# Grouped-query decode attention beside a mish layer: where the next pair's queries are spread, and which of VectorE's work stands first in the second unit

## The chip, the cores and the metric

The kernel runs on one core of one Trainium2 chip. The metric is device time in microseconds of one execution, the median of several runs. The profile is one execution more, taken by the hardware profiler.

## The reference

One decode step for 8 sequences of width 512. A layernormed input goes through cached attention with 32 query heads over 8 key/value heads (8192 cached positions, head size 128) and through a dense layer with mish; both are added to the input. All is float32.

```python
def _A_ref(x, k_cache, v_cache, wq, wo):
    q = (x @ wq).reshape(B, Sq, Hq, Dh).transpose(0, 2, 1, 3)
    k = jnp.repeat(k_cache, rep, axis=1)
    v = jnp.repeat(v_cache, rep, axis=1)
    scores = jnp.einsum("bhqd,bhkd->bhqk", q, k) * (Dh ** -0.5)
    p = softmax(scores, axis=-1)
    o = jnp.einsum("bhqk,bhkd->bhqd", p, v)
    return o.transpose(0, 2, 1, 3).reshape(B, Sq, Hq * Dh) @ wo

def _B_ref(x, w1, b1, w2):
    h = jnp.einsum("bsd,df->bsf", x, w1) + b1
    sp = jnp.log1p(jnp.exp(-jnp.abs(h))) + jnp.where(h > 0, h, jnp.zeros_like(h))
    return jnp.einsum("bsf,fd->bsd", h * jnp.tanh(sp), w2)

xn = layernorm(x)
return x + _A_ref(xn, ...) + _B_ref(xn, ...)
```

## The kernel before

The caches are the bulk: keys and values are 268 MB each, read once. The work is cut into 32 units. A unit is one sequence and one pair of key/value heads; a pair of heads has 8 units, one for each sequence, so there are 4 pairs. In the loop `j` is the unit, `b = j % 8` its place in the pair.

A unit's key tile and value tile are 8.39 MB each (128 partitions of 64 KB). They share one SBUF tile, `kv`, of 160 KB a partition. Values always lie at its start. Keys lie in two places that overlap by half: even units at `ROW`, odd units at `1.5 ROW`. So the keys of unit `j + 1` may be loaded only when the half of the keys of `j` that both places share has been used; `scores` therefore goes through that shared half first, and the load of the next keys is issued between the two halves of `scores`. All these loads go through SP's queue, in program order: the next keys wait for the first half of the scores, the next values for the values matmuls that still read the value place.

A unit runs in this order on each engine, as written in the loop (the order is by hand; the pools and the scheduler do not reorder it):

- `scores(j)`, line 279: 64 TensorE matmuls of a weight tile `wk` made from the queries against the keys, into one PSUM bank.
- `softmax(j)`, lines 291 to 312: row maximum on VectorE, two small TensorE transposes, the exponential on ScalarE, row sums.
- `values(j - 1)`, line 341: 64 TensorE matmuls of the previous unit's probabilities against its values, then four VectorE operations (lines 349 and 351) that gather the result.
- `key_weights(j + 1)`, line 262: two VectorE products that make the next unit's `wk` from the spread queries `qr`.
- `turn(j)`: TensorE matmuls (lines 318 and 319) that move the probabilities into four PSUM banks, then on VectorE the reciprocal (321), four transposes into `tr` (323) and two reduces into `pt8` (329).
- `merge(j - 1)`: one TensorE matmul (358) and a VectorE product (359).

Once in a pair the queries of the next pair are made: the weights are loaded at `b == 4` (`load_q`), projected at `b == 5` (`project`, lines 218 to 237), and spread. The spread is two steps: `selections` (line 205) copies a pattern from the identity into `wide`, which is the same memory as `tr`; `spread` (lines 244 and 251) runs two groups of 8 TensorE matmuls with that pattern as weights into two of the four PSUM banks that `turn` uses, each group followed by a ScalarE copy into `qr`. Before, both steps stand at the end of the unit with `b == 6`.

The first unit has no previous values. In their place it runs `mish`: TensorE matmuls (365, 370) and some 15 VectorE operations (378 to 404) that work in the memory in which the third unit's keys will be loaded.

Of the kernel before, what the change touches and what calls it, by code (L numbers as in the profile page):

```python
# [29 lines left out]
FG = F // G  # L30
# [26 lines left out]
W1_AT = ROW  # L57
# [1 line left out]
PLACES = 2 * ROW + ROW // 2  # L59


LOAD_Q, MAKE_Q, SPREAD_Q = 4, 5, 6


@with_exitstack
def kernel(
# [20 lines left out]
    kv = const.tile([P, PLACES], F32, name="kv")  # L87
# [26 lines left out]
    def load_q(m):  # L114

        rows = wq.rearrange("j p f -> (j p f)").rearrange("(m p f) -> m p f", m=NP, p=P)
        nc.sync.dma_start(ws, rows[m])

    def load_unit(src, j, at):
        m, b = divmod(j, B)  # L120
        lo = (b * HKV + 2 * m) * NH * G
        t = kv[:, at : at + ROW]
        nc.sync.dma_start(
            t,
            src[lo : lo + NB].rearrange("j p f -> (j p f)").rearrange("(p f) -> p f", p=P),
        )
        return t
# [5 lines left out]
    b1_sb = kv[:G, W1_AT + 7168 : W1_AT + 7168 + FG]  # L133
# [3 lines left out]
    w1_t = kv[:, W1_AT : W1_AT + 7168].rearrange("p (j f) -> p j f", j=2 * CC)  # L137
# [75 lines left out]
    def project():  # L213

        w = ws.rearrange("p (c f) -> p c f", c=CC)
        for d in range(2):
            for c in range(CC):
                nc.tensor.matmul(  # L218
                    H[Q * c : Q * c + B, :],
                    xn4[:, c, :],  # L220
                    w[:, c, d * 512 : (d + 1) * 512],
                    start=True,
                    stop=True,
                )
            qp = work.tile([P, 512], F32, name="e")
            nc.scalar.copy(qp, H)  # L226
            for h in range(REP):
                at = 192 + (d * REP + h) * B
                nc.tensor.matmul(  # L229
                    M[:, at : at + B],  # L230
                    qp[:, h * DH : (h + 1) * DH],
                    bsel[:, :B],
                    start=True,
                    stop=True,
                )
        qT = work.tile([P, H2 * B], F32, name="qT", bufs=1)
        nc.vector.tensor_scalar_mul(qT, M[:, 192 : 192 + H2 * B], DH**-0.5)
        return qT

    def spread(qT):  # L240

        for half in range(2):
            for k in range(8):
                nc.tensor.matmul(  # L244
                    X[:, half, k * 64 : (k + 1) * 64],
                    wide[:, half * 8 + k],
                    qT,
                    start=True,
                    stop=True,
                )  # L250
            nc.scalar.copy(  # L251
                qr[:, half * 8 : (half + 1) * 8].rearrange("p i c -> p (i c)"), X[:, half]
            )
# [3 lines left out]
    def key_weights(j):  # L257
        b = j % B
        w = WK[j] = work.tile([P, DI, 2, NH * G, REP], F32, name="wk", bufs=1)
        q = qr.rearrange("p i (d o h b) -> p i d o h b", d=2, o=1, b=B)[..., b]  # L260
        for d in range(2):
            nc.vector.tensor_mul(  # L262
                w[:, :, d],
                q[:, :, d].to_broadcast([P, DI, NH * G, REP]),
                mask[:, d * NH * G : (d + 1) * NH * G]
                .rearrange("p (o k r) -> p o k r", o=1, r=1)
                .to_broadcast([P, DI, NH * G, REP]),
            )


    def scores(j, k, first, part):

        w = WK[j]
        lo = 0 if first else DI // 2
        kk = k.rearrange("p (i c f) -> p i c f", i=DI, c=HALF)
        for n in range(DI // 2):
            i = lo + n
            for c in range(HALF):
                nc.tensor.matmul(  # L279
                    S[64 * c : 64 * (c + 1), :],  # L280
                    w[:, i].rearrange("p d k h -> p (d k h)"),
                    kk[:, i, c, :],
                    start=(part == 0 and n == 0),
                    stop=(part == 1 and n == DI // 2 - 1),
                )
# [51 lines left out]
    def values(j, vt):  # L337
        for n in range(NJ):
            l, c = divmod(n, HALF)
            q = n % G  # L340
            nc.tensor.matmul(  # L341
                O[Q * q : Q * (q + 1), :],
                pt8[:, c, TL * l : TL * (l + 1), :].rearrange("p t h -> p (t h)"),
                vt[:, 512 * n : 512 * (n + 1)],
                start=(n < G),
                stop=(n >= NJ - G),
            )
        os = work.tile([P, DH], F32, name="os")
        nc.vector.tensor_scalar(os, O[:, :DH], isel[:, 0:1], None, op0=ALU.mult)  # L349
        for i in range(1, TL):  # L350
            nc.vector.scalar_tensor_tensor(  # L351
                os, O[:, DH * i : DH * (i + 1)], isel[:, i : i + 1], os, op0=ALU.mult, op1=ALU.add
            )
        return os
# [7 lines left out]
    def mish(w1_t, b1_sb, flat):  # L362
        hp = H[:, :FG]
        for g in range(G):
            nc.tensor.matmul(
                hp[Q * g : Q * g + B, :], gsel[:, g, :], b1_sb, start=True, stop=False
            )
        for c in range(CC):
            for g in range(G):
                nc.tensor.matmul(  # L370
                    hp[Q * g : Q * g + B, :],
                    xnT[:, c, :],
                    w1_t[:, c * 2 + g // 2, g % 2 * FG : (g % 2 + 1) * FG],
                    start=False,
                    stop=(c == CC - 1),
                )
        a, z, z2, one, h = (flat[:, FG * i : FG * (i + 1)] for i in range(5))
        nc.vector.tensor_copy(h, hp)
        nc.vector.scalar_tensor_tensor(a, h, -1.0, h, op0=ALU.mult, op1=ALU.max)
        nc.scalar.activation(z, a, AF.Exp, scale=-1.0)  # L380
        nc.vector.tensor_mul(z2, z, z)
        m = a
        nc.vector.tensor_single_scalar(m, h, 0.0, op=ALU.is_gt)
        nc.vector.tensor_scalar(one, z2, -1.0, 1.0, op0=ALU.mult, op1=ALU.add)
        nc.vector.tensor_mul(one, one, m)
        t1 = m
        nc.vector.tensor_add(t1, one, z2)
        t2 = z2
        nc.vector.tensor_scalar(one, one, -1.0, 1.0, op0=ALU.mult, op1=ALU.add)
        nc.vector.scalar_tensor_tensor(t2, z, 2.0, t1, op0=ALU.mult, op1=ALU.add)  # L390
        nc.vector.scalar_tensor_tensor(t1, one, 2.0, t2, op0=ALU.mult, op1=ALU.add)
        nc.vector.reciprocal(z, t1)
        nc.vector.tensor_mul(t1, t2, z)
        act = one
        half = FG // 2
        for e in range(2):
            nc.vector.tensor_mul(
                act.rearrange("p (i a e l) -> p e a l i", a=2, e=2, i=W2R)[:, e],
                h[:, half * e : half * (e + 1)].rearrange("p (a l i) -> p a l i", a=2, i=W2R),
                t1[:, half * e : half * (e + 1)].rearrange("p (a l i) -> p a l i", a=2, i=W2R),  # L400
            )
        turned = flat[:, 5 * FG : 6 * FG]
        nc.vector.transpose(turned, act)
        nc.vector.tensor_copy(aT, turned.rearrange("p (j q) -> p j q", q=Q)[:, :, :B])
# [31 lines left out]
    qT = project()  # L436
# [4 lines left out]
    for j in range(UNITS):  # L441
        b = j % B
        more = j // B + 1 < NP

        k = k_t.pop(j)
        scores(j, k, j % 2 == 1, 0)
        if j == UNITS - 1:
            v_t[j] = load_unit(v, j, K_AT[0])
        elif j > 0:
            k_t[j + 1] = load_unit(kT, j + 1, K_AT[(j + 1) % 2])  # L450
        scores(j, k, j % 2 == 0, 1)
        WK.pop(j)
        lsel = softmax(j)
        os = None
        if j > 0:
            os = values(j - 1, v_t.pop(j - 1))
        else:
            mish(w1_t, b1_sb, kv[:, W1_AT : W1_AT + 6 * FG])
        if j + 1 < UNITS:
            v_t[j] = load_unit(v, j, V_AT)  # L460
            key_weights(j + 1)
        if more and b == LOAD_Q:
            load_q(j // B + 1)
        if more and b == MAKE_Q:
            qT = project()
        turn(j, lsel)
        if j > 0:
            merge(j - 1, os)
        if more and b == SPREAD_Q:
            selections()  # L470
            spread(qT)


    w_o = [kv[:, 4096 * m : 4096 * (m + 1)] for m in range(NP)]
# [72 lines left out]
```

## Time and profile before

| | us |
|---|---|
| median of 3 runs | 1332.83 |
| lowest and highest run | 1330.54, 1333.72 |
| profiled execution, its own time | 1329.46 |
| its span in the profile | 1327.7 |
| TensorE busy | 990.3 (75%) |
| VectorE busy | 514.8 (39%) |
| ScalarE busy | 40.2 (3%) |
| share of the span in which SP's queue moved data, mean of 16 DMA engines | 98.2% |

In the rows of the profile, PE is TensorE's matmuls, DVE is VectorE, ACT is ScalarE, SPq is the issue of a DMA on SP's queue. A row of the timeline has the start in us, the duration in us, the engine, the line, the operation, output and inputs, a count, and in brackets how long the engine stood idle before it and what it waited for. A row of the chain of waits has start, duration and what ran. In a row of stretches stand the stretch, its length, the busy time of each engine with the number of instructions, the granted TensorE clock as a share of full speed, the mean busy share of the DMA engines, and the GB/s.

### The profile page before, as it was taken

To read this page: it belongs to the slowest core of one execution; us is meant where nothing else is said; L and a number is where in the kernel's file an instruction comes from. 1 tells how busy PE (TensorE), PEld (TensorE's weight loads), DVE (VectorE), ACT (ScalarE), POOL (GpSimd) and SP (SyncE) were. 2 spreads that over 40 slices of the span, in tenths; PEclk is the share of its full clock that TensorE was granted. 3 is DMA by queue.
4 is the path that set the end of the run, shared out by engine and by line. 5 is a ranking of instruction groups with operands and counts; after the bars stand their busy time and mean duration, and the time that the engine had idled before them with its cause. 6 is when DMAs were issued, how large, how long until landed. Compare 5 with 4: busy or idle time off the path is not lost.

```text
span 1327.7 us, 11151 instructions
## 1 busy us (share of the span) xinstructions
PE 990.3 (75%) x5040; PEld 349.4 (26%) x5040; DVE 514.8 (39%) x728; ACT 40.2 (3%) x88; POOL 2.2 (0%) x9
## 2 busy tenths in 40 slices
PE   5688767878887678785877677788686687677666
PEld 3222222323222222233322222232332222222222
DVE  3464344431444433345243344413444423344421
ACT  1000000000000000000000000000000000000000
POOL 0000000000000000000000000000000000000000
PEclk9999888787988898877998788788697988888897
DMA  9999999998999999999999999999899999999998
GB/s 394 443 407 418 439 440 418 439 435 340 431 439 441 417 433 439 435 433 427 393 433 423 435 439 431 431 429 439 370 417 435 439 437 423 432 439 437 429 414 334
DMA packets 13591, 561.79 MB, mean 423 GB/s; under 512 B 1244, under 2 KB 1376, under 8 KB 4584
## 3 DMA queue, kind: packets, MB, share of 16 engines
q1 hardware_dynamic: 13520, 561.06, 98.2%
q8 instruction: 39, 0.64, 0.2%
q14 instruction: 8, 0.07, 0.0%
q10 hardware_dynamic: 24, 0.02, 0.0%
HBM read 561.01 MB, written 0.07 MB: 423 GB/s over the span
## 4 chain that ended last, share of the span: by engine, by line
DMA 65%; PE 29%; DVE 5%; ACT 1%; issue 0%; SPq 0%
DMA kv<-in_v 62%; PE o L341 19%; PE s L279 6%; DMA kv<-in_w 3%; PE x L244 2%; DVE pt L329 2%; PE x L318 1%; DVE tr L323 1%; DVE tr L205 0%; PE h L425 0%; DVE wk L262 0%; PE m L229 0%; PE h L218 0%; DVE nm L291 0%; PE h L370 0%
## 5 line engine op out<-in xcount | busy, mean ns | idle before, releaser
L279 PE MATMUL s<-kv,wk 128*64 128x512 f32 x2048 | 507.4, 659 | 165.7 <-DMA kv<-in_kT 153.1
L341 PE MATMUL o<-kv,pt 128*32 128x512 f32 x2048 | 258.5, 663 | 51.8 <-DMA kv<-in_v 42.2
L279 PEld LDWEIGHTS s<-kv,wk 128*64 128x64 f32 x2048 | 156.3, 152 | 491.6 <-issue 322.9
L329 DVE TENSOR_REDUCE pt<-tr 64x512 f32<-64x2048 f32 x64 | 241.4, 3771 | 1.6
L291 DVE TENSOR_REDUCE nm<-s 128x1 f32<-128x512 f32 x32 | 22.1, 692 | 413.5 <-PE s L279 413.5
L318 PE MATMUL x<-e,perm 128*128 128x512 f32 x256 | 126.7, 641 | 0.0
L341 PEld LDWEIGHTS o<-kv,pt 128*32 128x32 f32 x2048 | 68.2, 120 | 215.5 <-issue 161.2
L349 DVE TENSOR_SCALAR os<-o,isel 128x128 f32<-128x128 f32 x32 | 11.2, 351 | 261.1 <-PE o L341 261.1
L323 DVE STREAM_TRANSPOSE tr<-x 128x512 f32<-128x512 f32 x128 | 78.7, 673 | 0.0
L318 PEld LDWEIGHTS x<-e,perm 128*128 128x128 f32 x256 | 49.3, 203 | 75.1 <-issue 75.1
L262 DVE TENSOR_TENSOR wk<-qr,mask 128x512 f32<-128x512 f32 x64 | 62.9, 1023 | 8.7 <-ACT qr L251 8.7
L244 PE MATMUL x<-qT,tr 128*128 128x64 f32 x128 | 29.4, 424 | 37.7 <-DVE tr L205 34.7
L310 ACT ACTIVATE e<-s,nmx 128x512 f32<-128x512 f32 x32 | 22.0, 687 | 1058.0 <-DVE nmx L307 1058.0
L244 PEld LDWEIGHTS x<-qT,tr 128*128 128x128 f32 x128 | 27.9, 330 | 38.8 <-DVE tr L205 35.0
L351 DVE SCALAR_TENSOR_TENSOR os<-o,isel,os 128x128 f32<-128x128 f32 x96 | 33.7, 351 | 3.4
L292 PE MATMUL m<-ident,nm 128*1 128x128 f32 x32 | 8.6, 270 | 25.5 <-DVE nm L291 25.5
L303 PE MATMUL m<-ident,nx 1*128 1x1 f32 x32 | 7.0, 218 | 24.1 <-DVE nx L299 24.1
L358 PE MATMUL m<-hsel,os 128*128 128x8 f32 x64 | 12.4, 266 | 9.3 <-DVE rt L321 9.3
L312 DVE TENSOR_SCALAR lsel<-rsel,l 128x8 f32<-128x8 f32 x32 | 7.4, 231 | 30.4 <-ACT e L310 30.4
L321 DVE RECIPROCAL rt<-m 128x8 f32<-128x8 f32 x32 | 6.6, 207 | 29.7 <-PE m L319 29.7
L292 PEld LDWEIGHTS m<-ident,nm 128*1 128x1 f32 x32 | 2.5, 79 | 53.7 <-DVE nm L291 53.7
L229 PE MATMUL m<-bsel,e 128*128 128x8 f32 x64 | 11.8, 313 | 6.0 <-ACT e L226 6.0
(88 smaller groups left out, 165.7 us busy)
## 6 DMA issues: line engine op xcount, KB each, us to landing
ws<-in_wq SPq DMA_DIRECT2D x4, 2048.0 KB, 34.3
kv<-in_wo SPq DMA_DIRECT2D x4, 2048.0 KB, 24.3
kv<-in_w SPq DMA_DIRECT2D x1, 3584.0 KB, 26.6
kv<-in_w SPq DMA_DIRECT2D x1, 2048.0 KB, 35.6
kv<-in_w SPq DMA_DIRECT2D x1, 1024.0 KB, 20.7
kv<-in_kT SPq DMA_DIRECT2D x32, 29.6
kv<-in_v SPq DMA_DIRECT2D x32, 30.0
kv<-in_w SPq DMA_DIRECT2D x1, 512.0 KB, 20.5
```

The source lines that it names most:

```text
L229: nc.tensor.matmul(M[:, at : at + B], qp[:, h * DH : (h + 1) * DH], bsel[:, :B], start=True, stop=True,)
L244: nc.tensor.matmul(X[:, half, k * 64 : (k + 1) * 64], wide[:, half * 8 + k], qT, start=True, stop=True,)
L262: nc.vector.tensor_mul(w[:, :, d], q[:, :, d].to_broadcast([P, DI, NH * G, REP]), mask[:, d * NH * G : (d + 1) * NH * G] .rearrange("p (o ...
L279: nc.tensor.matmul(S[64 * c : 64 * (c + 1), :], w[:, i].rearrange("p d k h -> p (d k h)"), kk[:, i, c, :], start=(part == 0 and n == 0), s ...
L291: nc.vector.tensor_reduce(nm, S, axis=AX.X, op=ALU.max, negate=True)
L310: nc.scalar.activation(e, S, AF.Exp, bias=nmx, accum_out=l)
L318: nc.tensor.matmul(X[:, g], perm[:, g], e, start=True, stop=True)
L323: nc.vector.transpose(tr.rearrange("p (l t) c -> p t l c", t=TL)[:, tl], X.rearrange("p g (t q l) -> p t l g q", t=TL, q=PP)[:, tl],)
L329: nc.vector.tensor_reduce(pt8[half, :, :, d * REP : (d + 1) * REP].rearrange("p c y h -> p y c h"), tr[half].rearrange("p y (g c h) -> p y ...
L341: nc.tensor.matmul(O[Q * q : Q * (q + 1), :], pt8[:, c, TL * l : TL * (l + 1), :].rearrange("p t h -> p (t h)"), vt[:, 512 * n : 512 * (n ...
L351: nc.vector.scalar_tensor_tensor(os, O[:, DH * i : DH * (i + 1)], isel[:, i : i + 1], os, op0=ALU.mult, op1=ALU.add)
L358: nc.tensor.matmul(M[:, 168 : 168 + H2], os, hsel, start=True, stop=True)
```

## The change

The spread moves from the end of the unit with `b == 6` into the unit with `b == 7`, behind the matmuls of its values and the issue of its value load, and ahead of the key weights that need it. The selection copy stays at the end of the unit with `b == 6`. In the first unit, the value load and the key weights of the second unit are written ahead of `mish` instead of behind it; SP's order of loads is the same, and so is TensorE's order there, but VectorE's two products now stand ahead of its mish operations.

```diff
-LOAD_Q, MAKE_Q, SPREAD_Q = 4, 5, 6
+LOAD_Q, MAKE_Q, SPREAD_Q = 4, 5, 7
...
         os = None
         if j > 0:
             os = values(j - 1, v_t.pop(j - 1))
-        else:
-            mish(w1_t, b1_sb, kv[:, W1_AT : W1_AT + 6 * FG])
         if j + 1 < UNITS:
             v_t[j] = load_unit(v, j, V_AT)
+            if more and b == SPREAD_Q:
+                spread(qT)
             key_weights(j + 1)
+        if j == 0:
+            mish(w1_t, b1_sb, kv[:, W1_AT : W1_AT + 6 * FG])
         if more and b == LOAD_Q:
             load_q(j // B + 1)
         if more and b == MAKE_Q:
             ...
         turn(j, lsel)
         if j > 0:
             merge(j - 1, os)
-        if more and b == SPREAD_Q:
+        if more and b == SPREAD_Q - 1:
             selections()
-            spread(qT)
```

## The prediction

> **What bounds the kernel now.** I read the page's head first, then single stretches of the span, then the chain of waits, then the timeline around a pair's end.
>
> ```profile
> span 1327.7 us, 11151 instructions
> ...
> GB/s 394 443 407 418 439 440 418 439 435 340 431 439 441 417 433 439 435 433 427 393 433 423 435 439 431 431 429 439 370 417 435 439 437 423 432 439 437 429 414 334
> DMA packets 13591, 561.79 MB, mean 423 GB/s; under 512 B 1244, under 2 KB 1376, under 8 KB 4584
> ```
>
> Each of the 40 values is a slice of 33.2 us. Most are near 435 GB/s; the tenth (340), the twentieth (393) and the 29th (370) are low, and each lies where a pair of heads ends. Stretches, with the granted TensorE clock, the DMA share and the GB/s as last columns:
>
> ```profile
> 57.00:118.00 61.00, 43.38 (x211) 14.30 (x209) 36.98 (x48) 1.56 (x4) 0.00 (x0) 0.89 0.97 414
> ...
> 74.00:76.00 2.00, 2.00 (x12) 0.57 (x10) 2.00 (x1) 0.00 (x0) 0.00 (x0) 1.00 0.08 33
> 127.00:278.00 151.00, 114.19 (x536) 39.08 (x535) 61.11 (x84) 3.51 (x8) 0.00 (x0) 0.86 1.00 432
> 248.00:254.00 6.00, 6.00 (x12) 3.29 (x13) 0.23 (x1) 0.00 (x0) 0.00 (x0) 0.50 0.93 404
> 314.50:320.50 6.00, 6.00 (x28) 2.01 (x26) 0.00 (x0) 0.00 (x0) 0.00 (x0) 0.88 0.00 0
> 957.50:961.00 3.50, 3.50 (x20) 1.18 (x18) 0.00 (x0) 0.00 (x0) 0.00 (x0) 1.00 0.00 0
> ```
>
> Between pair ends the stream is full: 151 us at 432 GB/s with TensorE busy for 114. At the end of the first and third pairs it stands still for 6.0 and 3.5 us, and near 75 us, in the second unit, for about 2. So the kernel is a stream of key and value tiles, and it is late only where the queue is empty. 561.79 MB at 432 GB/s are 1300.4 us; the span is 27.3 us more.
>
> The Trainium skill's "DMA: Bandwidth & Descriptors", Specifications, names two ceilings, a fabric one of 435 GB/s and an HBM one of about 358 GB/s for a core. By the second the 561.79 MB would take 1569 us (an estimate from that page) and no reordering could help; the 432 GB/s above contradict it and agree with the first.
>
> The chain of waits gives the stream's step, since values of a unit start when their tile lands (start, duration, what):
>
> ```profile
> 278.29 8.77 PE o L341 x64
> ...
> 363.05 8.81 PE o L341 x64
> ...
> 600.34 7.07 PE o L341 x64
> ...
> 681.92 8.40 PE o L341 x64
> ...
> 919.27 8.77 PE o L341 x64
> ...
> 1002.85 10.06 PE o L341 x64
> ...
> 1041.57 7.12 PE o L341 x64
> ...
> 1235.13 7.12 PE o L341 x64
> ```
>
> From 1041.57 to 1235.13 are five units: 38.71 us each, one key and one value tile. Over a pair's end two units take 84.76, 81.58 and 83.58 us (363.05 - 278.29, 681.92 - 600.34, 1002.85 - 919.27). Less 77.42 that leaves 7.34, 4.16 and 6.16: together 17.66 us lost at the three pair ends.
>
> **Pair ends: what is removed.** The timeline from the sixth to the eighth unit of the first pair (units 5, 6, 7):
>
> ```profile
> 249.13 6.33 PE L318 MATMUL x<-e,perm 128*128 128x512 f32 x8
> ...
> 255.88 0.39 PE L358 MATMUL m<-hsel,os 128*128 128x8 f32 x2 [0.30 <-DVE rt L321]
> ...
> 258.94 16.80 PE L279 MATMUL s<-kv,wk 128*64 128x512 f32 x64 [2.67 <-DMA kv<-in_kT]
> ...
> 268.91 0.33 SPq L123 DMA_DIRECT2D kv<-in_kT  x1
> ...
> 286.99 3.70 PE L318 MATMUL x<-e,perm 128*128 128x512 f32 x8
> ...
> 301.13 1.88 DVE L205 COPY tr<-ident 128x2048 f32<-128x2048 f32 x1
> 303.07 3.67 PE L244 MATMUL x<-qT,tr 128*128 128x64 f32 x16 [11.56 <-DVE tr L205]
> ...
> 311.02 16.36 PE L279 MATMUL s<-kv,wk 128*64 128x512 f32 x64
> 311.13 0.59 ACT L251 COPY qr<-x 128x512 f32<-128x512 f32 x1 [3.77 <-PE x L244]
> 320.56 0.33 SPq L123 DMA_DIRECT2D kv<-in_kT  x1
> ```
>
> Unit 6 ends with the spread (L244): TensorE stands 11.56 us until VectorE has finished its reduces and the selection copy, then spreads, and only at 311.02 begins the scores of unit 7. The next key tile's issue stands behind the first half of those scores, so it goes at 320.56. The keys of unit 6 land at 258.94, the values of unit 5 at 278.29: 19.35 us a tile. So the keys of unit 7 land at 297.6 and the values of unit 6 at 317.0, and the issue comes 3.56 us after the queue ran dry. Two other such issues:
>
> ```profile
> 639.47 0.33 SPq L123 DMA_DIRECT2D kv<-in_kT  x1
> ...
> 960.20 0.33 SPq L123 DMA_DIRECT2D kv<-in_kT  x1
> ```
>
> By the same count the value tile ahead lands at 600.34 + 38.71 = 639.05 and 919.27 + 38.71 = 957.98, so these are late by 0.42 and 2.22. The losses 7.34, 4.16 and 6.16 are the lateness plus 3.78, 3.74 and 3.94. That is the rule of my sum: an issue costs 3.8 us less its lead on the landing of the tile ahead, and nothing once the lead is over 3.8.
>
> In the changed kernel the selection copy stays at the end of unit 6 and the spread goes behind the values matmuls of unit 7. Scores of unit 7 then wait for their keys alone, 297.6 instead of 311.02; as in unit 6 the issue follows 9.97 us later (268.91 - 258.94), at 307.6, with a lead of 9.4. The loss goes.
>
> **Pair ends: what is added, and what is late next.** Scores of unit 7 end at 297.6 + 16.80 = 314.4; values of unit 6 start on their landing at 317.0 and take 8.77, to 325.8. Their release issues the values of unit 7, with a lead of 10.5 us on the next pair's first keys (317.0 + 19.35 = 336.3). No DMA changes its place on SP, and POOL has none of this.
>
> Behind the values stands the spread: from 303.07 to the end of its second copy at 311.72 it takes 8.65, so to 334.4; its selection has been ready since 303. VectorE's key weights now wait there for ScalarE's copies instead of finding them done. Queued behind that wait on VectorE are the reciprocal, the transposes and reduces of unit 7 and the product of the merge; none of the transposes could run before, since turn's matmuls on TensorE also wait for the copies to free PSUM. Those matmuls start at 334.4. By the row at 249.13, also behind small matmuls, they take 6.33, and to the end of the merge 7.1 (255.88 + 0.39 - 249.13): the next scores start at 341.5. By the row at 286.99 they take 3.70, and the scores start at 338.9. Their keys landed at 336.3, so they are late by 2.6 to 5.2. Their issue follows 9.97 later, at 348.9 to 351.5, and the values ahead land at 355.7: a lead of 4.2 to 6.8, against 3.8 needed. So the spread moves from a place where it costs 4 to 7 us to one where it uses up slack and costs between nothing and, if another 1.0 us is late, 0.6 per pair.
>
> Which of the two durations holds is the clock: 248 to 254 us was granted 0.50 although TensorE was busy for all 6.00 us. The Trainium skill's "TensorE: Matmul & The Clock Gate", Part 1, has the clock fall to half after an idle window of about 3.4 us; around the moved spread TensorE pauses only for copies of 0.59 us, so by it the clock stays full, 3.70 holds and the lead is 6.8. The trace disagrees with it at the project of unit 5, and I go by the trace: 4.2.
>
> **The second unit.**
>
> ```profile
> 52.02 0.23 DVE L312 TENSOR_SCALAR lsel<-rsel,l 128x8 f32<-128x8 f32 x1 [2.19 <-ACT e L310]
> ...
> 57.08 0.28 PE L319 MATMUL m<-lsel,ones 128*128 128x8 f32 x2
> ...
> 65.15 0.22 DVE L404 COPY aT<-kv 128x112 f32<-128x112 f32 x1
> 65.28 1.92 DVE L262 TENSOR_TENSOR wk<-qr,mask 128x512 f32<-128x512 f32 x2
> ...
> 67.25 15.37 PE L279 MATMUL s<-kv,wk 128*64 128x512 f32 x64 [9.88 <-DVE wk L262]
> ...
> 69.79 7.56 DVE L329 TENSOR_REDUCE pt<-tr 64x512 f32<-64x2048 f32 x2
> ...
> 75.80 0.33 SPq L123 DMA_DIRECT2D kv<-in_kT  x1
> ...
> 82.67 0.69 DVE L291 TENSOR_REDUCE nm<-s 128x1 f32<-128x512 f32 x1 [5.33 <-PE s L279]
> ...
> 84.59 7.07 PE L341 MATMUL o<-kv,pt 128*32 128x512 f32 x64
> ```
>
> Scores of unit 1 wait 9.88 us for their key weights behind mish on VectorE, and the third key tile goes out at 75.80, as the stream dries. Moved ahead, the two products run from 52.25 to 54.2, and mish ends at most 1.92 later, at 67.3. TensorE is free at 57.4, and the second keys have landed by about 57 (the stream dries at about 76, less a tile). Scores start at 57.4; their first half takes 8.55 (75.80 - 67.25), to 66.0. The third key tile also overwrites mish's room and so goes out when mish ends, at 66 to 67.3: a lead of 9. VectorE's reduces end no later than before, at 77.35; the row maximum follows, and 1.92 behind it (84.59 - 82.67) the values, to 86.3, with a lead of 9 on the keys (95.4). What goes is the dip in the first stretch: 61 us at 414 instead of 432 GB/s are 2.54 us.
>
> **The sum.** 17.66 + 2.54 = 20.2 us. From below, the empty stretches alone that the rows show (6.0 + 3.5 + 2.0) are 11.5. I take 18.5, near the upper end: the losses are measured end to end, and 0.6 per pair is taken off for the small margin of the lead. The profiled execution took 1329.46, so it becomes 1311.0; the median of the runs, 1332.83, lies 3.37 above it, and the forecast stands on the median: 1314.3.
>
> **Rivals.**
> 1. *A new dry place.* The scores behind a pair's end start at 345.7 or later, 4.2 us after my later estimate, and the issue loses its lead: 3.8 x 3 = 11.4 given back, 8.8 gained, 1324.0. For it: the small margin at half clock. Against it: every step has a row.
> 2. *Slower, by the clock.* TensorE stays at half rate through the first unit of a new pair. Matmuls at half clock take 6.33 / 3.70 = 1.71 times as long. A unit's 16.36 + 8.77 + 3.70 us, about 29, become 49, 10.6 over the stream's 38.71. With 3.8 for the lead that is 14.4 a pair, 43.1 in all, less 20.2: 1355.7. It decides once the cost passes 6.7 a pair. Against it: after the half clock of 248 to 254, the scores at 258.94 took 16.80, no longer than the 16.36 at 311.02.
> 3. *The stream gives nothing back*: kept full for 1200 us instead of 300, it runs 1.5% slower, and the time stays 1332.8. Against it: five full units late in the run still take 38.71 each.
>
> **Chances.** Forecast 0.86, new dry place 0.07 (still faster), slower by the clock 0.04, no gain 0.03. A change of 0.3%, 4 us, is about what a measurement of this kernel can tell from none. Faster 0.93, same 0.03, slower 0.04. The range: from above, 1332.83 - 11.5 = 1321; from below, 1332.83 - 20.2, and as the runs shown scatter down to 1330.54, 3 to 4 us under that: 1309.
>
> **What would show it.** In the changed profile the wait of L244 for L205 is gone, the three low slices are near 430, two units over a pair's end take 77.4 to 79, the key issue near 320 comes near 307, and the one at 75.80 near 66. I am wrong if a stretch without traffic appears 40 us later, behind the spread, or if the granted clock is 0.5 through a whole unit.

## The result, and the profile after

The changed kernel takes 1313.41 us (median of 4 runs, 1312.52 to 1313.82) against 1333.28 for the kernel before (median of 4, 1330.54 to 1334.18) on the same chip. The ratio is 0.9861, with a 95% interval of 0.9844 to 0.9879. The forecast was 1314.3 us, in a range of 1309 to 1321.

The head of the page after, its slices, and its row for the spread:

```profile
span 1311.7 us, 11148 instructions
...
GB/s 393 450 422 439 428 434 431 430 444 428 432 432 434 428 440 424 440 426 434 432 428 446 416 442 430 430 440 422 438 430 436 430 430 432 436 424 438 426 418 313
...
L244 PE MATMUL x<-qT,tr 128*128 128x64 f32 x128 | 19.3, 315 | 3.0 <-ACT qr L251 2.7
```

The three low slices of the kernel before (340, 393, 370) have become ordinary ones, and between the first slice and the last two none is below 416. The spread no longer waits for VectorE's copy of line 205; what is left is 2.7 us in total for ScalarE's copies. Stretches of the changed kernel (the last columns are granted clock, DMA share, GB/s):

```profile
57.00:118.00 61.00, 46.26 (x224) 15.86 (x228) 34.66 (x46) 1.55 (x4) 0.00 (x0) 0.87 1.00 432
314.50:320.50 6.00, 4.79 (x24) 1.20 (x28) 0.23 (x1) 0.32 (x2) 0.00 (x0) 0.50 0.93 404
324.00:330.00 6.00, 5.33 (x48) 3.94 (x40) 1.40 (x4) 0.58 (x1) 0.00 (x0) 1.00 0.91 393
100.00:1200.00 1100.00, 834.99 (x4160) 283.08 (x4156) 431.00 (x594) 28.80 (x68) 0.00 (x0) 0.87 1.00 432
```

The stream now runs for 1100 us at the 432 GB/s that it had between pair ends before. The dip of the second unit (414) is gone too. The chain of waits, at the places that answer to those of before:

```profile
275.75 8.81 PE o L341 x64
...
354.43 9.19 PE o L341 x64
...
547.98 7.12 PE o L341 x64
...
593.10 8.81 PE o L341 x64
...
670.51 9.87 PE o L341 x64
...
825.34 8.81 PE o L341 x64
...
865.59 7.12 PE o L341 x64
...
909.19 7.12 PE o L341 x64
...
986.61 8.81 PE o L341 x64
```

Two units over a pair's end take 78.68, 77.41 and 77.42 us, where they took 84.76, 81.58 and 83.58: the losses of 7.34, 4.16 and 6.16 are now 1.26, 0 and 0. The 1.26 lies in the first of the two steps, from 275.75 to the next values at 315.71 (39.96 us instead of 38.71), and so not behind a late issue; it is taken up with the sum below. The timeline of the first pair's end, unit 7 and the start of unit 8:

```profile
295.10 16.67 PE L279 MATMUL s<-kv,wk 128*64 128x512 f32 x64 [6.13 <-DMA kv<-in_kT]
...
304.95 0.33 SPq L123 DMA_DIRECT2D kv<-in_kT  x1
...
325.37 2.00 PE L244 MATMUL x<-qT,tr 128*128 128x64 f32 x16
...
328.04 2.00 PE L244 MATMUL x<-qT,tr 128*128 128x64 f32 x16 [0.68 <-ACT qr L251]
330.07 0.58 ACT L251 COPY qr<-x 128x512 f32<-128x512 f32 x1 [2.09 <-PE x L244]
330.71 3.70 PE L318 MATMUL x<-e,perm 128*128 128x512 f32 x8 [0.68 <-ACT qr L251]
...
335.16 13.95 PE L279 MATMUL s<-kv,wk 128*64 128x512 f32 x64
...
342.29 0.33 SPq L123 DMA_DIRECT2D kv<-in_kT  x1
```

Scores of unit 7 now wait for their own keys (6.13 us, released by the DMA), the issue of the next keys comes at 304.95 instead of 320.56, and the values ahead land at 275.75 + 38.71 = 314.5: a lead of 9.5 where there was a lateness of 3.56 (10.8 by 315.71, at which these values did start). The spread takes its place behind the values. And in the second unit:

```profile
51.33 1.96 DVE L262 TENSOR_TENSOR wk<-qr,mask 128x512 f32<-128x512 f32 x2
...
57.79 13.95 PE L279 MATMUL s<-kv,wk 128*64 128x512 f32 x64 [1.24 <-DVE kv L387]
...
64.69 0.22 DVE L404 COPY aT<-kv 128x112 f32<-128x112 f32 x1
...
64.98 0.33 SPq L123 DMA_DIRECT2D kv<-in_kT  x1
```

The third key tile goes out at 64.98 instead of 75.80, as soon as mish has left its room; the first half of the scores is done at about the same time.

### The profile page after: what moved, and what is told of

Its sections match the earlier page's. It is cut to its first block, busy times and chain, and to the rows that moved or that the text cites. A ratio compares the mean times of both kernels' runs of the same rounds, so it can differ in the third digit from the quotient of the medians.

```text
span 1311.7 us, 11148 instructions
## 1 busy us (share of the span) xinstructions
PE 985.5 (75%) x5040; PEld 341.1 (26%) x5040; DVE 515.0 (39%) x728; ACT 40.2 (3%) x88; POOL 2.2 (0%) x9
## 2 busy tenths in 40 slices
DMA packets 13591, 561.79 MB, mean 428 GB/s; under 512 B 1244, under 2 KB 1376, under 8 KB 4584
## 4 chain that ended last, share of the span: by engine, by line
DMA 73%; PE 23%; DVE 2%; issue 0%; ACT 0%; SPq 0%; DVEq 0%
DMA kv<-in_v 71%; PE o L341 20%; DMA kv<-in_w 3%; PE s L279 1%; DVE pt L329 1%; PE x L244 1%; PE h L425 0%; PE m L229 0%; PE h L218 0%; PE h L370 0%; DVE kv L392 0%; DVE tr L323 0%; DVE wk L262 0%; DVE nm L291 0%; ACT L177 0%
## 5 line engine op out<-in xcount | busy, mean ns | idle before, releaser
L341 PE MATMUL o<-kv,pt 128*32 128x512 f32 x2048 | 269.9, 687 | 56.0 <-DMA kv<-in_v 46.4
L244 PE MATMUL x<-qT,tr 128*128 128x64 f32 x128 | 19.3, 315 | 3.0 <-ACT qr L251 2.7
L244 PEld LDWEIGHTS x<-qT,tr 128*128 128x128 f32 x128 | 18.1, 226 | 6.2 <-ACT qr L251 3.3
L319 PEld LDWEIGHTS m<-lsel,ones 128*128 128x128 f32 x64 | 12.2, 190 | 15.4 <-issue 15.2
```

The costliest lines, as they stand in the source:

```text
L244: nc.tensor.matmul(X[:, half, k * 64 : (k + 1) * 64], wide[:, half * 8 + k], qT, start=True, stop=True,)
L319: nc.tensor.matmul(M[:, 136 : 136 + H2], ones, lsel, start=True, stop=True)
L341: nc.tensor.matmul(O[Q * q : Q * (q + 1), :], pt8[:, c, TL * l : TL * (l + 1), :].rearrange("p t h -> p (t h)"), vt[:, 512 * n : 512 * (n ...
```

## The experiments

The theory under test is that of the prediction: the time is the stream of tiles plus what is lost wherever its queue runs dry; a key issue costs 3.8 us less its lead on the tile ahead, and nothing once the lead is larger. Two chips beside the first were used; the kernel before took 1330.36 us on the one (17 runs), where the first four experiments ran, and 1331.43 on the other (13 runs), where the delays ran.

**The spread alone.** The first unit is as before, the spread moved.

```diff
         if j > 0:
             os = values(j - 1, v_t.pop(j - 1))
+        else:
+            mish(w1_t, b1_sb, kv[:, W1_AT : W1_AT + 6 * FG])
...
-        if j == 0:
-            mish(w1_t, b1_sb, kv[:, W1_AT : W1_AT + 6 * FG])
```

> The changed kernel with mish back ahead of the second unit's key weights, so that only the spread has moved. Theory (each place where the queue of loads runs dry costs its own time, and the two parts add): the three pair ends give their 17 to 18 us back and the dip near 75 us stays, so about 1316, 2.5 above the changed kernel's 1313.4; the key issue of the second unit stays near 75.8 us and the stretch 57 to 118 us at about 414 GB/s. Rival (an earlier stream is taken up by slack at the next pair end, so that one part alone brings all or nothing): 1313 or 1333.

Measured: 1316.76 us, ratio 0.9897 (0.9877 to 0.9916). The stretch of the second unit, in its profile:

```profile
57.00:118.00 61.00, 44.88 (x211) 14.60 (x209) 36.63 (x48) 1.56 (x4) 0.00 (x0) 0.86 0.97 412
```

And from its chain:

```profile
279.58 7.12 PE o L341 x64
...
356.98 8.52 PE o L341 x64
```

The dip stays and the pair ends are cured: two units over the first take 77.40 us (78.92 and 78.95 over the others, with a long step of 40.2 in each, of the kind named with the sum below). Of the gain, 13.6 is the spread's.

**The key weights alone.** The other half: mish behind the second unit's key weights, the spread at its old place.

```diff
-        else:
-            mish(w1_t, b1_sb, kv[:, W1_AT : W1_AT + 6 * FG])
         if j + 1 < UNITS:
             v_t[j] = load_unit(v, j, V_AT)
             key_weights(j + 1)
+        if j == 0:
+            mish(w1_t, b1_sb, kv[:, W1_AT : W1_AT + 6 * FG])
```

> The kernel before with only the second unit's key weights moved ahead of mish. Theory: the dip near 75 us goes (2.5 us), the three pair ends stay, so about 1330.5; the key issue of the second unit comes at about 65 us and the issues at the pair ends stay late by up to 4 us. Rival (what is gained in the second unit is given back at the first pair end, where the stream waits for the scores and not the scores for the stream): 1333, with a longer empty stretch near 315 us.

Measured: 1327.33 us, ratio 0.9973 (0.9959 to 0.9986), 3.0 us less (by the interval, 1.9 to 5.5). Its stretch of the second unit and one at the first pair's end, then the issues there:

```profile
57.00:118.00 61.00, 46.41 (x224) 15.77 (x228) 34.67 (x46) 1.55 (x4) 0.00 (x0) 0.87 1.01 435
315.00:317.50 2.50, 2.50 (x16) 0.77 (x12) 0.00 (x0) 0.00 (x0) 0.00 (x0) 1.00 0.00 0
```

```profile
64.98 0.33 SPq L123 DMA_DIRECT2D kv<-in_kT  x1
...
316.78 0.33 SPq L123 DMA_DIRECT2D kv<-in_kT  x1
```

The dip is gone, the empty stretch at the pair's end is there, and what the second unit gained is not taken back there. The parts add: 13.6 + 3.0 = 16.6, against 16.9 for both on this chip (1330.36 to 1313.47, the next run, which holds both, with the selection copy late).

**The selection late.** In the changed kernel the selection copy goes behind the values as well, so that TensorE waits for VectorE again, at the new place.

```diff
             if more and b == SPREAD_Q:
+                selections()
                 spread(qT)
...
-        if more and b == SPREAD_Q - 1:
-            selections()
```

> The changed kernel with the selection copy also moved, directly ahead of the spread in the last unit of a pair, so TensorE waits there for VectorE again, for the gathering of the values and the copy: 1.5 + 1.9 us. Theory (an issue costs nothing while its lead on the tile ahead is over 3.8 us): the lead of the key issue behind the spread falls from 12 to about 8.5 us and the time stays 1313.4. Rival (what counted was taking VectorE's work from TensorE's path, wherever it stands): 3.4 us at each of three pair ends, about 1323.

Measured: 1313.47 us, ratio 0.9872 (0.9852 to 0.9892), the same as the changed kernel. From its timeline:

```profile
315.27 7.07 PE L341 MATMUL o<-kv,pt 128*32 128x512 f32 x64 [1.98 <-DMA kv<-in_v]
...
325.77 2.56 PE L244 MATMUL x<-qT,tr 128*128 128x64 f32 x16 [3.42 <-DVE tr L205]
...
346.85 0.33 SPq L123 DMA_DIRECT2D kv<-in_kT  x1
```

The wait for L205 is back, 3.42 us at this pair's end, and costs nothing, because the issue that stands behind it still has a lead: 315.27 + 38.71 - 346.85 = 7.1, where 8.5 was expected (5.8 and 4.4 at the other two pair ends, where two units lost 0.3 each). A wait on TensorE is not a loss by itself; it is one if it takes the lead of an issue below some 4 us.

**The old place with a pattern of its own.** The kernel before, mish first, the spread still at the end of unit 6; the pattern is copied in unit 5 into the idle buffer of the query weights.

```diff
+    late = ws[:, : DI * P].rearrange("p (i o) -> p i o", i=DI)
...
             qT = project()
+            selections(late)
...
         if more and b == SPREAD_Q:
-            selections()
-            spread(qT)
+            spread(qT, late)
```

> The kernel before with the spread at its old place, the end of the seventh unit, and mish first, but with the pattern copied one unit earlier into memory of its own (the idle buffer of the query weights) instead of the memory of the transposes. So the spread no longer waits for VectorE's reduces and copy. Theory (the price was the 11.6 us wait, and the spread itself fits in TensorE's wait for the keys): the spread starts about 2 to 3 us behind the merge and ends near 300, the next key issue comes near 309, with a lead of over 3.8, and the pair ends lose nothing: about 1316. Rival (the spread's own 5 to 9 us on TensorE at that place are the price): the issue comes near 315 and at least half of the 17.7 us stays lost, 1324 or more.

Measured: 1317.25 us, ratio 0.9904 (0.9886 to 0.9923), as much as moving the spread. From its timeline (its lines are numbered two higher):

```profile
279.26 7.07 PE L343 MATMUL o<-kv,pt 128*32 128x512 f32 x64 [1.44 <-DMA kv<-in_v]
...
292.75 2.05 PE L246 MATMUL x<-qT,ws 128*128 128x64 f32 x16 [1.98 <-DVE tr L325]
...
307.34 0.33 SPq L123 DMA_DIRECT2D kv<-in_kT  x1
```

The spread waits 1.98 us for the transposes instead of 11.56 for reduces and copy, and the issue has a lead of 279.26 + 38.71 - 307.34 = 10.6. So the price at the old place was not the spread but the late copy of its pattern, which stood behind VectorE's reduces because it used the memory of the transposes.

**A delay of known size.** In the changed kernel 6, 12 or 18 matmuls of no use are put ahead of a new pair's first scores. They change no result.

```diff
             merge(j - 1, os)
+        if more and b == SPREAD_Q:
+            for _ in range(18):
+                nc.tensor.matmul(H, perm[:, 0], perm.rearrange("p g q -> p (g q)"), start=True, stop=True)
```

> The changed kernel itself, as the foot of the three that follow: 1313.4 by every theory.

> The changed kernel with 6 idle-work matmuls (128x512, into an unused PSUM bank, of no use to the result) on TensorE at the end of each pair's last unit, ahead of the next pair's first scores: about 0.93 us each, 5.6 us in all. It lowers the lead of the key issue that follows from about 12 to 6.5 us. Theory (cost = 3.8 us less the lead, never below nothing): no cost, 1313.4. Rival 1 (TensorE's work at a pair end is on the path): 3 x 5.6 more, 1330. Rival 2 (a late issue costs only its lateness): no cost either.

> The same with 12 such matmuls, about 11.1 us: the lead falls to about 1 us. Theory: 2.8 us at each of three pair ends, about 1322. Rival 1: 3 x 11.1, 1347. Rival 2 (a late issue costs only its lateness, so nothing while the lead is positive): 1313.4.

> The same with 18 such matmuls, about 16.7 us: the issue is late by about 4.6 us. Theory: 8.4 us at each pair end, about 1339. Rival 1: 3 x 16.7, 1363. Rival 2: 4.6 at each pair end, about 1327.

Measured: 1312.58 us without, 1312.73 with 6, 1319.34 with 12, 1329.99 with 18 (ratios to the kernel before 0.9854, 0.9854, 0.9904 and 0.9987, the last from 0.9972 to 1.0002). From the chain and the DMA issues of the kernel with 6, at the first pair's end:

```profile
315.39 8.39 PE o L341 x64
...
392.80 8.81 PE o L341 x64
```

```profile
348.89 0.33 SPq L123 DMA_DIRECT2D kv<-in_kT  x1
```

Of the kernel with 18, at the first two pair ends, and its timeline for the matmuls themselves:

```profile
315.44 8.58 PE o L341 x64
...
400.20 8.81 PE o L341 x64
...
637.59 7.07 PE o L341 x64
...
721.08 8.81 PE o L341 x64
```

```profile
357.83 0.33 SPq L123 DMA_DIRECT2D kv<-in_kT  x1
...
678.58 0.33 SPq L123 DMA_DIRECT2D kv<-in_kT  x1
```

```profile
655.82 15.70 PE L473 MATMUL h<-perm 128*128 128x512 f32 x36
```

And of the kernel with 12, at the first and third:

```profile
315.43 8.39 PE o L341 x64
...
396.76 8.75 PE o L341 x64
...
951.48 7.07 PE o L341 x64
...
1030.97 8.81 PE o L341 x64
```

```profile
354.10 0.33 SPq L123 DMA_DIRECT2D kv<-in_kT  x1
...
987.20 0.33 SPq L123 DMA_DIRECT2D kv<-in_kT  x1
```

The lead is the first start plus 38.71 less the issue, the loss the two units' time less 77.42:

| kernel, pair end | lead, us | loss, us | 3.8 less lead |
|---|---|---|---|
| 6, first | 5.2 | 0.0 | 0 |
| 12, third | 2.99 | 2.07 | 0.8 |
| 12, second | 2.91 | 1.50 | 0.9 |
| 12, first | 0.04 | 3.91 | 3.8 |
| 18, second | -2.28 | 6.07 | 6.1 |
| 18, first | -3.68 | 7.34 | 7.5 |

(At the second pair's end of the kernel with 12 the starts are 633.88 and 712.80 and the issue is at 669.68.) At the pair ends that are not in the table, leads of 6.1 and 7.9 lost 0.1 and 0.0 (6), and one of -2.31 lost 6.05 (18). The rule holds within 0.2 us except near its corner: at leads of 2.9 and 3.0 the loss is 0.6 and 1.3 more than the rule has it. TensorE's work as such is not on the path (rival 1: 6 of them would have cost 17 us), and a late issue does not cost its lateness alone (rival 2: nothing at a lead of 0.04, where 3.91 was lost). The times for 12 and 18 were forecast too high, 1322 and 1339, because of the size of the delay, not of the rule: 18 matmuls took 15.70 us and not 16.7, and the values ahead of the second spread took 7.07 instead of the 8.8 they mostly take in the changed kernel, so the issue was late by 2.28 instead of 4.6.

## Why the prediction was right

*The bound.* Right: 561.79 MB at 432 GB/s, with the queue full, set the time, and only dry places could be won back.

*What is removed at the pair ends.* Right in mechanism and size. Forecast was an issue at 307.6 with a lead of 9.4; it came at 304.95 with 9.5. Of 17.66 us, 16.4 went, and the 1.26 that is left is not behind a late issue.

*What is late next.* Too pessimistic. The spread with its copies was put at 8.65 us, from rows of before; it took 5.28 (325.37 to the end of the copy at 330.65). The turn's matmuls were put at 6.33; they took 3.70 at the first and third pair's end, and at the second

```profile
645.78 5.17 PE L318 MATMUL x<-e,perm 128*128 128x512 f32 x8 [0.68 <-ACT qr L251]
```

The first half of the scores took 7.1 (335.16 to 342.29, granted a clock of 1.00), not 9.97 (258.94 to 268.91 of the kernel before, granted 0.71). The lead came to 12.1 (354.43 - 342.29) instead of 4.2, so the 0.6 us a pair taken off for a thin margin was not needed. The error is the clock. In the kernel before, the spread's rows of 3.67 us stand in this stretch:

```profile
300.00:311.00 11.00, 7.26 (x32) 6.97 (x32) 2.98 (x3) 0.59 (x1) 0.00 (x0) 0.50 1.00 435
```

It was granted 0.50 there, after 11.56 us without work. In the changed kernel the spread follows 9.72 us of values, has 1.00 (the stretch 324 to 330 above), and its halves take 2.00. So a duration was carried from a cold place to a warm one. The rule of the Trainium skill's "TensorE: Matmul & The Clock Gate", Part 1, which the prediction weighed and set aside, has the clock fall to half after an idle window of about 3.4 us. The trace agrees with it at the first pair's end (granted 1.00 from 324 to 342.29) and at the third (1.00 from 957 to 975), where TensorE paused for at most 0.8 us at a time. It disagrees at the second, where the pauses were as short and the turn's matmuls of 5.17 us above stand in this stretch:

```profile
645.78:651.00 5.22, 5.22 (x10) 2.45 (x10) 1.94 (x2) 0.00 (x0) 0.00 (x0) 0.71 0.99 427
```

From 645.40 to 648.80 the clock was 0.50 there; in the 3.40 us before, TensorE had been busy for 2.43. So the full clock was the better guess, but not a certain one; the lead at that pair's end was still 11.7.

*The second unit.* Right: 64.98 against 66 to 67.3 forecast, and the stretch from 414 to 432 GB/s. Alone it measured 3.0 us, against 2.54. Mish ended no later than before (64.91 against 65.37), where up to 1.92 later was allowed for.

*The sum.* 18.5 forecast. By medians it was 19.9 on the first chip, 16.9 and 18.9 on the two others; by the two profiled spans 16.0. In the two chains the pair ends and the second unit give 16.4 + 2.5 = 18.9. Against that stand single steps in the full stream that are some 1.5 us too long: 865.59 - 825.34 = 40.25, and 593.10 - 547.98 = 45.12, where a step with query weights took 43.60 before. With a third (1102.73 to 1142.95, 40.22) and the 39.96 from 275.75 to 315.71 they come seven units apart. The chain of before has one in the full stream (1235.13 to 1275.32, 40.19). Three less one are 3.1 us, and 18.9 - 3.1 = 15.8 is close to the 16.0 of the spans. What makes the long steps was not tried; it stays open. The prediction had no term for them, and its deduction for the margin, 0.6 a pair, covered part of them by chance. That the median came within 0.9 us of the forecast is luck to that extent: one deduction was not needed, one term was missing, and the four runs of before alone spread over 3.6 us.

*The rivals.* No new dry place appeared (no issue lost its lead), the clock did not stay at half, and the stream kept its rate over 1100 us. The prediction's row against a half clock did not show what it was used for: 16.80 is longer than 16.36, and the first half of those scores was granted 0.71.

## What to carry to other kernels

Where a stream of loads sets the time, price a wait by the lead that the next load's issue still has, not by its own length: here 11.56 us of waiting cost 4 to 7, and 3.42 us at a place with slack cost nothing. Ask what memory a small step shares with what is ahead of it; a pattern of its own would have done as much as moving the step. Take a duration for a moved step from a row with the granted clock of the new place, and allow for another: it was 1.00 behind the moved spread at two pair ends and 0.71 at one.

## What the runs showed that was not expected

An issue must be early, not only in time: one that came 0.04 us ahead of the landing still lost 3.91 us, and nothing was lost from a lead of 5.2.

The same 128x64 matmuls took 2.00 us in a group of 16 at a granted clock of 1.00 and 3.67 at 0.50; a step behind a long wait is dear twice.

The runs of the kernel before scatter over 1327.7 to 1336.6 us on the two later chips, those of the changed kernel and its near relations without a dry place over 1312.3 to 1313.9. In one profile of before, three equal pair ends lose 7.34, 4.16 and 6.16, by issues that are late by 3.56, 0.42 and 2.22. The trace shows where they differ. The values took 8.77, 7.07 and 8.77 us (granted clock 0.81, 1.00, 0.81), and the first half of the scores 9.54, 8.09 and 8.20 (311.02 to 320.56, 631.38 to 639.47, 952.00 to 960.20; 0.74, 0.88, 0.87). The 24.0 us between the two are the same to 0.01. So the lateness differs by what TensorE's two groups took, and they took longer where the granted clock was lower. The scatter of the runs fits that, but what sets the clock at a pair's end was not tried.
